# The rounding of the sequence table on VectorE, the square-root table behind the first casts, and a cast in contiguous order: relu²-attention with Fourier mixing on one core

## The chip, the cores and the metric

The kernel runs on one core of a Trainium2 chip. The metric is the device time of one execution in microseconds (us). The kernel before takes 571.43 us, the median of three runs (570.71 to 571.96 us).

## The reference, cut to what matters

```python
def _attn_ref(q, k, v):                       # (8, 12, 448, 64) each
    scores = scale * np.matmul(q, k.transpose(0, 1, 3, 2))
    attn = np.maximum(scores, 0.0) ** 2 / S   # S = 448
    return np.matmul(attn, v)

def _moe_ref(x, w_ch1, w_ch2):                # x: (8, 448, 768), w: 768x3072, 3072x768
    mixed = np.real(np.fft.fft(np.fft.fft(x, axis=1), axis=2))
    u = x + mixed
    un = (u - mean(u)) / np.sqrt(var(u) + 1e-06)      # over the last axis
    return u + np.maximum(un @ w_ch1, 0.0) @ w_ch2
```

`x` is the attention output, with the twelve heads side by side in the last axis. The real part of the two Fourier transforms is computed as matrix products with tables of cosines and sines, one table along the channels (768) and one along the sequence (448).

## The kernel before, in words

**Staging.** The eight batches run through one software pipeline. For each batch: attention (scores L954 on TensorE, relu on ScalarE at L967, squares on VectorE at L984 or on ScalarE at L981, products with v at L822 and L827), the transposed attention output `xT` copied out of PSUM (L673 for batch 0, L689 for the others), sums and differences of mirrored sequence positions (`fold`, L748 for batch 0, L727 to L780 later), the product with the channel table (`mix`, L1407 for batch 0 and L1432 later), the casts of its result to `pc` (L1451), the product with the sequence table (L1029 and L1032 for batch 0; L1244 for batch 1 and L1240 for the later ones), layernorm, and the two layers of the channel network (first layer L1928, its relu on VectorE L1913 or ScalarE L1915 into `hT`; second layer L1956, L1983 and L2069, whose result VectorE adds to the output at L1621). From some batches on, the network runs with pre-added blocks (L2045 to L2057), which saves products.

**Tables.** The sequence table is made at run time in `seq_table` and `seq_sines`: GpSimd (POOL) forms position times frequency over 448 (L366), rounds it to the nearest whole number (L369) and takes the fraction (L371); VectorE takes the absolute value (L377); ScalarE makes cosines and sines of it (three instructions, L383) into `seq` (`seqm` in the profile) and `nseq`. `root_table` (L399) is a square root of a constant whose purpose is to bring ScalarE's table of the square root in at a chosen place: the ACT_TABLE_LOAD in front of it is the cost. `halve` (L407 to L411) multiplies the table with a permutation on TensorE and casts the result into `half_seq` (`seqh`), whose even and odd columns stand in two blocks.

**The order of the work.** `Streams.run` lays the program out while it is built. Each piece of work is a generator that asks for its next step with `need(engine, duration, what it waits for, buffers)`; the planner takes the step that can start first by its own model, with an added rank and small corrections by phase (`HEAD`), and issues it. What the engines then do on the chip is in exactly that order on each engine, whatever the real durations are. So a changed duration or constant in the model can move instructions anywhere later. Loads from memory are issued by POOL (software queue, L451, L476 for q, k and v; L515 and L526 for the weights, shown as `w<-in_moe_w_ch_dram`), relayouts, transposes and stores by SyncE (SP).

Of the kernel before, what the change touches and what calls it, by code (L numbers as in the profile page):

```python
# [13 lines left out]
ALU = mybir.AluOpType  # L14
# [47 lines left out]

HEAD = {('attentions', 'PE', 2): -0.6, ('attentions', 'PE', 3): -0.6}
OVERLAP = {"ACT": 0.12, "DVE": 0.07}
STAGE = [1]
LATENCY = {"PE": 0.28, "ACT": 0.18, "DVE": 0.16, "POOL": 0.2, "SP": 0.1}
# [89 lines left out]
def act(n):  # L158
    return n / 1200 + (0.17 if STAGE[0] else 0.2)
# [18 lines left out]
def kernel(  # L178
# [174 lines left out]
    def seq_table():  # L353

        f = work.tile([128, 4 * KH], FP32, name="dfty", tag="uA", bufs=1)
        g = work.tile([128, 4 * KH], FP32, name="dfty", tag="uB", bufs=1)
        yield need("POOL", 0.55)
        nc.gpsimd.iota(drow[:, 0:2], pattern=[[128, 2]], base=0, channel_multiplier=1,
                       allow_small_or_imprecise_dtypes=True)
        nc.gpsimd.iota(dcol[:, 0:SX], pattern=[[1, SX]], base=0, channel_multiplier=0,  # L360
                       allow_small_or_imprecise_dtypes=True)
        yield need("POOL", 0.3)
        nc.gpsimd.tensor_scalar(drow[:, 0:2], drow[:, 0:2], 1.0 / S, None, op0=ALU.mult)
        for i in range(2):
            yield need("POOL", 0.45)
            nc.gpsimd.tensor_scalar(f[:, i * SX:(i + 1) * SX], dcol[:, 0:SX], drow[:, i:i + 1], None, op0=ALU.mult)  # L366
        f, g = f[:, 0:2 * SX], g[:, 0:2 * SX]
        yield need("POOL", 0.75)
        nc.gpsimd.tensor_scalar(g, f, ROUND, -ROUND, op0=ALU.add, op1=ALU.add)  # L369
        e = yield need("POOL", 1.1)  # L370
        nc.gpsimd.tensor_tensor(f, f, g, op=ALU.subtract)  # L371
        sch.add(seq_sines(f, g, e + LATENCY["POOL"]), (0, 0.3))

    def seq_sines(f, g, e):

        e = yield need("DVE", 0.4, [e])
        nc.vector.tensor_scalar(g.bitcast(mybir.dt.int32), f.bitcast(mybir.dt.int32), 0x7FFFFFFF, None,  # L377
                                op0=ALU.bitwise_and)
        flat = seq.rearrange("p t a s -> p t (a s)")
        for dst, y, sign, bias in ((flat[:, 0], g, -1, halfpi), (flat[:, 1], f, 1, zero_t),  # L380
                                   (nseq.rearrange("p a s -> p (a s)"), f, -1, zero_t)):
            e = yield need("ACT", act(2 * SX), [e + LATENCY["DVE"], last_relu])
            nc.scalar.activation(dst, y, AF.Sin, bias=bias, scale=sign * 2.0 * math.pi)  # L383
        seq_ready.t = nseq_ready.t = dft_ready.t = e + LATENCY["ACT"]

    ROUND = 1.5 * 2 ** 23
    chan_made, dft_made = [Cell() for _ in range(3)], Cell()

    def negative():
# [5 lines left out]

    def root_table():

        yield need("ACT", 1.5, [dft_ready, last_relu])
        nc.scalar.activation(drow[:, 7:8], zero_t, AF.Sqrt, bias=eps_t)  # L399

    def halve():

        yield need("SP", 0.0, [tail_left])
        e = yield need("PE", mm(2 * SX), [], [BS])
        pt = BS.take()
        for t in range(2):
            nc.tensor.matmul(pt[:2 * EH, t, 0:SX], lhsT=order[0][:EV, 0:2 * EH], rhs=seq[:EV, t, 0, :],  # L407
                             start=True, stop=True)
        e = yield need("DVE", 1.1, [e + LATENCY["PE"]], [BQR])
        half_seq[0] = work.tile([128, 2, 2, EV], BF16, name="seqh", tag="warm", bufs=1)  # L410
        nc.vector.tensor_copy(half_seq[0][:2 * EH].rearrange("p t o s -> p t s o"),  # L411
                              pt[:2 * EH, :, 0:2 * EV].rearrange("p t (s o) -> p t s o", o=2))
        BS.give(pt, e)
        BQR.free.append(e)
        half_ready.t = e + LATENCY["DVE"]

    GRP = 4 * R * HG * Dh * 4
    TURNED, STORED, RELAYED = 1.0, 1.0, 0.0
    loads = [[None] * 3 for _ in range(B * NG)]
    ready = [[Cell() for _ in range(3)] for _ in range(B * NG)]  # L420
    BQ = [[Bufs(1) for _ in range(QN)] for _ in range(2)] + [Bufs(3)]
# [12 lines left out]
    def arrive(i, x):  # L434

        arrived.setdefault((i, x), []).append(landed[-1])
        if len(arrived[i, x]) == (1, 2, 2)[x]:
            ready[i][x].t = max(arrived[i, x]) + (1.5 if i % NG else 0.0, 3.0, 6.0, 8.0)[min(i // NG, 3)]

    def load_halves(b, g, n, x):  # L440

# [205 lines left out]
    def fold(b, m, F, av, give, av_end):  # L647
# [4 lines left out]
        def leave():  # L652
# [10 lines left out]
            if b == 0:  # L663
                bufs = [BX[m]] + ([BA[m]] if m < 3 else [])
                wait = {x: max(av_end, sch.engine[x]) + sch.queued(x) for x in ("ACT", "DVE")}
                en = "ACT" if m in (3, 4) and wait["ACT"] + 2 * act(HS) < wait["DVE"] + 2 * dve(HS) else "DVE"
                for out_, in_ in (xa, xb):
                    t = yield need(en, act(HS) if en == "ACT" else dve(HS), [av_end], bufs)
                    bufs = []
# [290 lines left out]
    def squares(b, scs, sqs):  # L960
        for i, sc, t in scs:
            e = yield need("ACT", act(2 * S) - (0.0 if STAGE[0] else 0.03), [t + LATENCY["PE"]], [BSQ])
            at = min(sq_ids)
            sq_ids.remove(at)
            r = sqs[i][0] = work.tile([128, 2, S], BF16, name="sq", tag=f"sq{at[1]}", bufs=1)
            sqs[i][2] = at[1]
            nc.scalar.activation(r, sc[:, :, 0:S], AF.Relu)  # L967
            BS.give(sc, e + 0.1)
            if b == 0 and i == NB - 1:
                last_relu.t = e  # L970
            sch.add(square(b, r, e + LATENCY["ACT"], sqs[i][1]), (0.2, 0.2))

    def sooner(t, other, d, usual, du):

        wait = {en: max(t, sch.engine[en]) + sch.queued(en) for en in (other, usual)}
        return wait[other] + d + SPARE < wait[usual] + du

    def square(b, r, t, done):
        if b >= ELASTIC[0] and sooner(t, "ACT", act(2 * S), "DVE", dve2(2 * S)):
            e = yield need("ACT", act(2 * S), [t])  # L980
            nc.scalar.activation(r, r, AF.Square)  # L981
        else:
            e = yield need("DVE", dve2(2 * S), [t])
            nc.vector.tensor_tensor(r, r, r, op=ALU.mult)  # L984
        done.t = e + LATENCY["DVE"]
# [430 lines left out]
    def mix(b):  # L1416
# [23 lines left out]
            BFS.free.append(e)  # L1440
        for (n0, n1), (pp, t) in zip(TC, pps):
            n = n1 - n0 if b < PAR else 2 * EH
            en, copy = ("ACT", nc.scalar.copy) if n0 == 0 or b == 1 else ("DVE", nc.vector.tensor_copy)
            pc = None

            for w in ((slice(0, 1), slice(1, 2)) if b == 0 else (slice(0, 2),)):
                e = yield need(en, dve((w.stop - w.start) * 2 * KH), [t], [BPC] if n0 == 0 and w.start == 0 else [])
                if pc is None:
                    pc = work.tile([128, 2, 2 * KH], BF16, name="pc", tag=f"pc{n0}", bufs=1)

                copy(pc[:n, w].rearrange("p t (k r) -> p t r k", r=2),  # L1451
                     pp[:n, w, 0:2 * KH].rearrange("p t (r k) -> p t r k", r=2))
            BS.give(pp, e)
            pcs.append((pc, e + LATENCY["ACT"]))
        if b == 0:
            yield need("PE", 0.0, [], [BUNT, BUNT])
            for t0, n in ((0, 384), (384, 512)):
# [696 lines left out]
            begun = True  # L2154

    LEAD, MIXED, SPARE, ELASTIC = 2.9, 1, 0.5, (1, 99)
    SLOPE = 0.1
    with tc.manual_schedule():
        small_constants()
        sch.engine.update(POOL=0.5, DVE=2.6)  # L2160
# [52 lines left out]
```

## Time and profile before

| | |
|---|---|
| three timed runs | 570.71, 571.43, 571.96 us |
| profiled execution | 572.91 us, its span 571.1 us |
| granted TensorE clock | 1.000 |
| busy: PE, DVE, ACT, POOL | 558.0, 440.3, 317.7, 202.4 us |
| share of the chain that ended last | PE 90%, DVE 3%, DMA 2%, ACT 2% |

PE is TensorE, DVE is VectorE, ACT is ScalarE, POOL is GpSimd, SP is SyncE; the span runs from the first instruction to the last of the profiled execution. L numbers are lines of the kernel before. In rows of the timeline and of the chain the first column is the start in us from the span's start, the second a length; in rows of a table by stretches the first number is the stretch, the second its length, then the busy time of PE, PEld (weight loads), DVE, ACT and POOL with their instructions, the granted clock, the DMA share and GB/s.

### The profile page before, as it was taken

What the parts mean: (1) busy time and instruction counts of PE and PEld (TensorE: products, weight loads), DVE (VectorE), ACT (ScalarE), POOL (GpSimd) and SP (SyncE); (2) the same over time, 40 slices, a digit from 0 to 9 for tenths busy, and PEclk for the clock granted to TensorE, in tenths of its full rate; (3) what the DMA queues carried; (4) which work ended last, traced back from release to release, by engine and by line L of the source; (5) the groups of instructions that cost most, each with busy time, mean ns of one, the idle gap of its engine ahead of it and who ended that gap; (6) DMA issues with size and microseconds to landing.
All of it is one profiled execution on the core that took longest, in us unless ns stands there. A gap on an engine that the chain in (4) does not pass through costs nothing.

```text
span 571.1 us, 11283 instructions
## 1 busy us (share of the span) xinstructions
PE 558.0 (98%) x4240; PEld 353.1 (62%) x4240; DVE 440.3 (77%) x1019; ACT 317.7 (56%) x530; POOL 202.4 (35%) x284
## 2 busy tenths in 40 slices
PE   8989999999999999997999999999999999999997
PEld 6466546644465455555756766756668688668864
DVE  6977675887788978886998897888799967644762
ACT  5967772667645687585686647728515164005400
POOL 8987225524346234462455536325006000000000
PEclk9999999999999999999999999999999999999999
DMA  9999999989969998899999999956415421332012
GB/s 113 172 199 237 186 218 182 253 113 117 195 90 213 214 128 176 149 188 182 163 133 208 198 130 193 173 120 169 106 64 155 120 96 20 78 117 65 1 55 84
DMA packets 152689, 82.43 MB, mean 144 GB/s; under 512 B 118076, under 2 KB 147900, under 8 KB 152636
## 3 DMA queue, kind: packets, MB, share of 16 engines
q0 software_dynamic: 57056, 33.63, 43.5%
q1 hardware_dynamic: 95580, 48.09, 38.3%
q8 instruction: 33, 0.54, 0.4%
q14 instruction: 20, 0.16, 0.1%
HBM read 62.91 MB, written 26.25 MB: 156 GB/s over the span
## 4 chain that ended last, share of the span: by engine, by line
PE 90%; DVE 3%; DMA 2%; ACT 2%; POOL 1%; issue 1%; SPq 0%; DVEq 0%; POOLq 0%; ACTq 0%
PE psF L1928 27%; PE psF L2069 21%; PE psS L1760 8%; PE psS L954 7%; PE psS L2069 5%; PE psF L827 5%; PE psF L1956 4%; PE psF L1983 4%; PE psS L1432 2%; PE psF L1760 2%; PE psF L822 1%; DMA qk<-in_k_dram 1%; DVE sq L984 1%; DMA qkT<-qkr 1%; PE psS L827 1%; PE psS L1029 1%
## 5 line engine op out<-in xcount | busy, mean ns | idle before, releaser
L1928 PE MATMUL psF<-unT,w 128*128 128x256 bf16 (+2 forms) x1152 | 165.4, 299 | 1.1 <-DVE hT L1913 0.9
L967 ACT ACTIVATE sq<-psS 128x896 bf16<-128x896 f32 x168 | 144.4, 919 | 33.2 <-PE psS L954 32.8
L1928 PEld LDWEIGHTS <-w 128*128 128x128 bf16 x1152 | 110.9, 98 | 50.9 <-issue 6.7
L984 DVE TENSOR_TENSOR sq<-sq 128x896 bf16<-128x896 bf16 x143 | 88.8, 638 | 11.5 <-ACT sq L967 10.7
L2069 PEld LDWEIGHTS <-hT 128*128 128x128 bf16 x648 | 62.5, 98 | 43.6 <-issue 3.9
L1915 ACT ACTIVATE hT<-psF 128x512 bf16<-128x512 f32 (+2 forms) x118 | 58.0, 507 | 42.7 <-PE psF L1928 41.9
L1621 DVE TENSOR_TENSOR o<-psF,o 128x384 f32<-128x384 f32 (+1 forms) x78 | 42.6, 547 | 24.3 <-PE psF L2069 19.4
L2069 PE MATMUL psF<-w,hT 128*128 128x384 bf16 x336 | 60.1, 326 | 0.7 <-DVE o L1621 0.6
L954 PE MATMUL psS<-qkT 64*128 64x448 bf16 (+1 forms) x336 | 51.7, 354 | 3.4 <-DVE pc L1451 2.3
L1775 ACT COPY copies<-psS 128x256 f32<-128x256 f32 x57 | 19.9, 374 | 53.9 <-PE psS L1760 48.8
L1275 POOL TENSOR_TENSOR u<-tp,xn 112x385 f32<-112x385 f32 (+2 forms) x14 | 14.5, 1038 | 81.5 <-DVE tp L1255 62.0
L689 DVE TENSOR_SCALAR xT<-psF 128x224 bf16<-128x224 f32 x62 | 21.2, 384 | 23.2 <-PE psF L827 23.2
L476 POOL DMA_DIRECT2D qn<-in_q_dram x21 | 15.6, 742 | 59.3 <-DVE qkr L583 52.3
L954 PEld LDWEIGHTS <-qkT 64*128 64x128 bf16 (+1 forms) x336 | 13.1, 94 | 35.3 <-issue 29.0
L827 PE MATMUL psF<-sq,vn 128*64 128x448 bf16 x246 | 32.6, 362 | 0.0
L1760 PEld LDWEIGHTS <-w 128*128 128x128 bf16 x288 | 28.2, 98 | 4.7 <-issue 1.0
L1284 DVE BATCH_NORM_STATS2 stats<-u 112x6 f32<-112x384 f32 (+2 forms) x56 | 28.5, 542 | 0.9 <-POOL u L1275 0.6
L451 POOL DMA_DIRECT2D kn<-in_k_dram x42 | 25.7, 622 | 9.6 <-PE psF L1928 8.5
L476 POOL DMA_DIRECT2D vn<-in_v_dram x24 | 19.0, 797 | 27.7 <-PE psS L954 27.4
L451 POOL DMA_DIRECT2D vn<-in_v_dram x42 | 26.0, 632 | 7.9 <-DMA w<-in_moe_w_ch_dram 7.0
L1303 ACT ACTIVATE un<-u,small 113x768 bf16<-113x768 f32 (+2 forms) x21 | 20.9, 1023 | 10.9 <-DVE small L1290 8.3
L1780 DVE CUSTOM_DVE_ANT_0 hT<-psS,copies 128x256 bf16<-128x256 f32 x37 | 15.0, 421 | 14.1 <-PE psS L1760 6.2
(238 smaller groups left out, 961.7 us busy)
## 6 DMA issues: line engine op xcount, KB each, us to landing
out_dram<-o SPq DMA_DIRECT2D x55, 192.0 KB, 3.6
qn<-in_q_dram POOLq DMA_DIRECT2D x21, 224.0 KB, 5.2
vn<-in_v_dram POOLq DMA_DIRECT2D x24, 192.0 KB, 5.9
w<-in_moe_w_ch_dram POOLq DMA_DIRECT2D x12, 384.0 KB, 8.3
w<-in_moe_w_ch_dram POOLq DMA_DIRECT2D x4, 1152.0 KB, 20.5
kn<-in_k_dram POOLq DMA_DIRECT2D x21, 192.0 KB, 6.1
utop<-u SPq DMA_DIRECT2D x12, 336.0 KB, 3.1
o<-utop SPq DMA_DIRECT2D x16, 192.0 KB, 3.4
```

The source lines that it names most:

```text
L451: nc.gpsimd.dma_start(out=t[par * Dh:(par + 1) * Dh, par::2], in_=at)
L476: nc.gpsimd.dma_start(out=to, in_=src[b, hs, 0:rows].rearrange("h (p j) d -> p h (j d)", j=j))
L827: nc.tensor.matmul(av[h * Dh:(h + 1) * Dh, 0:S], lhsT=vn_home[:, at:at + Dh], rhs=sq[:, h, :], start=start, stop=stop, skip_group_check=True)
L954: nc.tensor.matmul(sc[:, h, 0:S].rearrange("k (c q) -> k c q", c=4), lhsT=flat[ps, k0:k0 + KB], rhs=qT[ps, pair], start=True, stop=True)
L967: nc.scalar.activation(r, sc[:, :, 0:S], AF.Relu)
L984: nc.vector.tensor_tensor(r, r, r, op=ALU.mult)
L1284: nc.vector.bn_stats(stats[:n, hf, :], u[:n, hf * (D // 2):(hf + 1) * (D // 2)])
L1621: nc.vector.tensor_tensor(o[:, cols], pc[:, cols], o[:, cols], op=ALU.add)
L1760: nc.tensor.matmul(ps[:, 0:N], lhsT=lhs, rhs=rhs[:, m], start=(start and m == 0), stop=(stop and m == 2), skip_group_check=True)
L1915: nc.scalar.activation(hs, ps, AF.Relu)
L1928: nc.tensor.matmul(ph[:, i * N:(i + 1) * N], lhsT=w1_sb[m][hf][:, (jj + i) * 128:(jj + i + 1) * 128], rhs=unT[:, m, 0:N], start=(m == 0), ...
L2069: nc.tensor.matmul(pc[:, cols], lhsT=lhs[i], rhs=rhs[i][:, cols], start=(start and i == 0), stop=(i == KP - 1), skip_group_check=True)
```

## The change

1. **Rounding.** POOL's two instructions (L369, L371) are gone. VectorE gets two in their place, ahead of the absolute value: the fraction's source is written as int32 (which rounds it), and the difference is taken (L373 and L375 of the kernel after).
2. **ScalarE takes two pieces of batch 0** from VectorE: the last square (L984 to L981) and the last `xT` (m = 5, L673 to L671).
3. **The square-root table** is loaded after the first `pc` cast, not before it.
4. **`halve`** casts with the destination in contiguous order; the source is then read in steps of two elements. Before, the source was contiguous and the destination was written in steps of 113 elements.
5. **Batch 1's second `pc` cast** (97 rows) goes to VectorE; both were on ScalarE.
6. **Constants of the planner** change, and with them the order on all engines.

```diff
-HEAD = {('attentions', 'PE', 2): -0.6, ('attentions', 'PE', 3): -0.6}
+HEAD = {('attentions', 'PE', 2): -0.6, ('attentions', 'PE', 3): -0.6, ('attentions', 'PE', 4): 0.07, ('mix_rows', 'PE', 2): -0.05}
...
 def seq_table():
...
-            yield need("POOL", 0.45)
+            e = yield need("POOL", 0.45)
...
-        yield need("POOL", 0.75)
-        nc.gpsimd.tensor_scalar(g, f, ROUND, -ROUND, op0=ALU.add, op1=ALU.add)
-        e = yield need("POOL", 1.1)
-        nc.gpsimd.tensor_tensor(f, f, g, op=ALU.subtract)
...
 def seq_sines(f, g, e):
         e = yield need("DVE", 0.4, [e])
+        nc.vector.tensor_scalar(g.bitcast(mybir.dt.int32), f, 1.0, None, op0=ALU.mult)
+        yield need("DVE", 0.55)
+        nc.vector.tensor_tensor(f, f, g.bitcast(mybir.dt.int32), op=ALU.subtract)
+        e = yield need("DVE", 0.4)
...
 def root_table():
-        yield need("ACT", 1.5, [dft_ready, last_relu])
+        yield need("SP", 0.0, [dft_ready, last_relu, first_copied])
+        yield need("ACT", 1.5, [first_copied])
...
 def halve():
-        e = yield need("DVE", 1.1, [e + LATENCY["PE"]], [BQR])
+        e = yield need("DVE", dve(4 * EV), [e + LATENCY["PE"]], [BQR])
-        nc.vector.tensor_copy(half_seq[0][:2 * EH].rearrange("p t o s -> p t s o"),
-                              pt[:2 * EH, :, 0:2 * EV].rearrange("p t (s o) -> p t s o", o=2))
+        nc.vector.tensor_copy(half_seq[0][:2 * EH], pt[:2 * EH, :, 0:2 * EV].rearrange("p t (s o) -> p t o s", o=2))
...
-    TURNED, STORED, RELAYED = 1.0, 1.0, 0.0
+    TURNED, STORED, RELAYED = 1.367, 1.225, 0.203
...
-            ready[i][x].t = max(arrived[i, x]) + (1.5 if i % NG else 0.0, 3.0, 6.0, 8.0)[min(i // NG, 3)]
+            ready[i][x].t = max(arrived[i, x]) + (1.5 if i % NG else 0.0, 2.944, 4.08, 8.038)[min(i // NG, 3)]
...
-                en = "ACT" if m in (3, 4) and wait["ACT"] + 2 * act(HS) < wait["DVE"] + 2 * dve(HS) else "DVE"
+                en = "ACT" if m == MC - 1 or m in (3, 4) and wait["ACT"] + 2 * act(HS) < wait["DVE"] + 2 * dve(HS) else "DVE"
...
-    def square(b, r, t, done):
-        if b >= ELASTIC[0] and sooner(t, "ACT", act(2 * S), "DVE", dve2(2 * S)):
+    def square(b, r, t, done, scalar):
+        if scalar or b >= ELASTIC[0] and sooner(t, "ACT", act(2 * S), "DVE", dve2(2 * S)):
...
-            en, copy = ("ACT", nc.scalar.copy) if n0 == 0 or b == 1 else ("DVE", nc.vector.tensor_copy)
+            en, copy = ("ACT", nc.scalar.copy) if n0 == 0 else ("DVE", nc.vector.tensor_copy)
...
-    SLOPE = 0.1
+    SLOPE = 0.127
```

The new order, at three places. **ScalarE in the head of the program**, from the end of batch 0's attention to the first rows of its layernorm (`sq` are attention weights, `seqm` and `nseq` the sequence table, `pc` the casts of the channel product). Before:

```order
L967 ACTIVATE sq<-psS 128x896
L383 ACTIVATE seqm<-dfty,few 128x480 x2
L383 ACTIVATE nseq<-dfty,few 128x480
L399 ACT_TABLE_LOAD
L399 ACTIVATE drow<-few 128x1
L1451 CAST pc<-psS 128x2x193 x2
L630 COPY qkT<-psF 128x960
L1081 COPY u<-psS 128x384
```

and with the change:

```order
L967 ACTIVATE sq<-psS 128x896
L981 ACTIVATE sq<-sq 128x896
L383 ACTIVATE seqm<-dfty,few 128x480
L671 ACTIVATE xT_108<-psF 128x224 x2
L383 ACTIVATE seqm<-dfty,few 128x480
L383 ACTIVATE nseq<-dfty,few 128x480
L1451 CAST pc<-psS 128x2x193 x2
L630 COPY qkT<-psF 128x960
L400 ACT_TABLE_LOAD
L400 ACTIVATE drow<-few 128x1
L1081 COPY u<-psS 128x384
```

The square and the two halves of `xT` have come in, and the table load has moved behind the casts and the copy of `qkT`, in front of the first copy of the rows.

**VectorE where batch 1's channel product ends** (`qkr` are q and k of batch 2 on their way to a transpose, `pc` the second cast, `o` the output's accumulator). Before:

```order
L740 TENSOR_TENSOR fold<-fold,seqm 128x450
L583 COPY qkr<-qn 112x1024
L1621 TENSOR_TENSOR o<-psF,o 128x384
L583 COPY qkr<-kn 128x1024
L1255 TENSOR_TENSOR tp<-psS,qs 128x385
```

and with the change (L1623 is L1621 of before):

```order
L740 TENSOR_TENSOR fold<-fold,seqm 128x450
L583 COPY qkr<-qn 112x1024
L1451 CAST pc<-psS 97x2x2x193
L1623 TENSOR_TENSOR o<-psF,o 128x384
L583 COPY qkr<-kn 128x1024
L1255 TENSOR_TENSOR tp<-psS,qs 128x385
```

The cast has come in behind the copy of q and ahead of the add into the output.

**VectorE ahead of the channel product L1432 that stands at 368.5 us in the trace of before** (`fold` and `diff` are what that product reads; `hT` are blocks of the network). Before:

```order
L770 TENSOR_TENSOR fold<-folds 128x684
L778 TENSOR_TENSOR diff<-fold 128x1368
L984 TENSOR_TENSOR sq<-sq 128x896
L780 TENSOR_TENSOR fold<-fold 128x1368
L984 TENSOR_TENSOR sq<-sq 128x896
L2045 TENSOR_TENSOR hT<-hT 128x512
```

and with the change (L2047, L2049, L2051 and L1623 are L2045, L2047, L2049 and L1621 of before):

```order
L778 TENSOR_TENSOR diff<-fold 128x1368
L984 TENSOR_TENSOR sq<-sq 128x896
L2047 TENSOR_TENSOR hT<-hT 128x256
L2049 TENSOR_TENSOR hT<-hT 128x256
L2051 TENSOR_TENSOR hT<-hT 128x2x128
L1623 TENSOR_TENSOR o<-psF,o 128x384
L780 TENSOR_TENSOR fold<-fold 128x1368
```

The last fold of the batch now stands behind the network's block additions and behind one add into the output. On TensorE the same place holds two dozen products L2069 ahead of L1432 that stood behind it before, and twelve L1928 that stood just ahead of it have moved up by some 8 us.

More of the change, by code (lines that the diff above doesn't have):

```diff
@@ L384, in seq_sines @@
         seq_ready.t = nseq_ready.t = dft_ready.t = e + LATENCY["ACT"]
-    ROUND = 1.5 * 2 ** 23
+    first_copied = Cell()
     chan_made, dft_made = [Cell() for _ in range(3)], Cell()
@@ L970, in squares @@
                 last_relu.t = e
-            sch.add(square(b, r, e + LATENCY["ACT"], sqs[i][1]), (0.2, 0.2))
+            sch.add(square(b, r, e + LATENCY["ACT"], sqs[i][1], b == 0 and i == NB - 1), (0.2, 0.2))
     def sooner(t, other, d, usual, du):
@@ L1454, in mix @@
             pcs.append((pc, e + LATENCY["ACT"]))
+            if b == 0 and en == "ACT":
+                first_copied.t = e
         if b == 0:
```

## The prediction

> **What bounds the kernel now.** I read four views in this order: the busy times by stretches, TensorE's waits, the chain of work that ended last, and the timeline at the places that the change touches. The table by stretches shows where TensorE (first busy number) isn't full.
>
> ```profile
> 60.00:93.00 33.00, 32.78 (x236) 17.88 (x236) 19.54 (x48) 22.23 (x33) 6.21 (x10) 1.00 1.25 197
> 93.00:257.00 164.00, 163.80 (x1040) 84.72 (x1039) 136.78 (x323) 106.70 (x168) 73.92 (x98) 1.00 1.04 168
> 257.00:270.00 13.00, 10.09 (x82) 6.35 (x79) 7.63 (x15) 6.84 (x8) 2.03 (x3) 1.00 1.23 177
> ```
>
> ```profile
> 359.00:410.00 51.00, 50.89 (x408) 34.57 (x406) 43.95 (x97) 31.98 (x48) 14.02 (x16) 1.00 0.77 143
> ```
>
> From 60 to 257 us TensorE is idle for 0.42 us of 197, from 359 to 410 for 0.11. No work leaves TensorE with this change, so only its waits can go or come. Two of the longest lie where the change acts:
>
> ```profile
> PE psS L1029 <- ACT pc L1451: 1.3, 1, 1.3
> ```
>
> ```profile
> PE psF L1928 <- DVE hT L1913: 0.9, 1, 0.9
> ```
>
> They stand at 36.7 and 52.6 us, as the rows below show. What is idle from 257 to 270 us (13.00 - 10.09 = 2.9) belongs to an order that the change leaves alone.
>
> **The head, up to 60 us.** The sequence table is late, and everything waits behind it. POOL rounds, VectorE's absolute value comes next, then ScalarE's sines, its table load and the casts that TensorE waits for:
>
> ```profile
> 28.78 1.84 POOL L369 TENSOR_SCALAR dfty<-dfty 128x480 f32<-128x480 f32 x1
> 30.71 1.48 POOL L371 TENSOR_TENSOR dfty<-dfty 128x480 f32<-128x480 f32 x1
> ```
>
> ```profile
> 32.24 0.40 DVE L377 TENSOR_SCALAR dfty<-dfty 128x480 int32<-128x480 int32 x1
> ```
>
> ```profile
> 32.67 1.28 ACT L383 ACTIVATE seqm<-dfty,few 128x480 bf16<-128x480 f32 x2 [2.77 <-DVE dfty L377]
> 33.86 0.68 ACT L383 ACTIVATE nseq<-dfty,few 128x480 bf16<-128x480 f32 x1
> 34.56 1.28 ACT L399 ACT_TABLE_LOAD   x1
> 35.85 0.29 ACT L399 ACTIVATE drow<-few 128x1 f32<-128x1 f32 x1
> 36.05 1.03 ACT L1451 CAST pc<-psS 128x386 bf16<-128x386 f32 x2
> 36.93 0.97 ACT L630 COPY qkT<-psF 128x960 bf16<-128x960 bf16 x1
> ```
>
> VectorE's two new instructions don't exist in this trace. The rounding has the shape of L377, 0.40 us; the difference has two inputs, and I take 0.6 us from the add L1621 over 384 elements (0.56 us, quoted below). Bounds are 0.4 for each and POOL's own 1.84 and 1.48. Three instructions at about 1.4 us, begun near 30.1 us behind the folds of the first three tiles, end at 31.5 instead of 32.64. The sines then start 1.1 us earlier; the two halves of the last `xT`, new between them on ScalarE, give back some 0.65. The added square falls into ScalarE's 2.77 us of idling, at
>
> ```profile
> L981 ACT ACTIVATE sq<-sq 128x896 bf16<-128x896 bf16 x25 | 23.6, 954 | 0.4
> ```
>
> 0.95 us, so it costs nothing; without that cover it would delay the sines by as much. With the load and the root (1.57) out of the way, the casts begin near 34.2 instead of 36.05 (36.05 - 1.1 + 0.65 - 1.57 = 34.03, and 0.17 for handoffs): **1.85 us earlier**. VectorE's half of the casts follows the folds, and two `xT` halves in front of them are gone.
>
> But the load is not gone. It now stands behind the copy L630, ahead of the first copy of a row tile, and TensorE's row tiles are filled and emptied in turn:
>
> ```profile
> 38.48 0.48 ACT L1081 COPY u<-psS 128x384 f32<-128x384 f32 x1 [0.58 <-DVE stats L1052]
> ```
>
> ```profile
> 36.68 0.94 PE psS L1029 x4
> 37.62 0.17 PE psS L1032 x3
> 37.79 0.66 PE psS L1029 x4
> 38.45 0.17 PE psS L1032 x3
> ```
>
> Casts until 35.2, L630 until 36.15, load and root until 37.75: the first L1081 ends near 38.25, where the profile has 38.96. The first three row tiles (0.66 + 0.17 = 0.83 us each) don't need it; the fourth, which began at 36.68 + 1.11 + 2 x 0.83 = 39.45, does. So it comes 1.2 us earlier and not 1.85, and I put the rows' gain at **1.1 us**.
>
> The Trainium skill (ScalarE: Activation LUTs, "What ACT_TABLE_LOAD costs") puts a switch at 1283 ns for the load plus about 1380 ns of drain. The row of the load agrees with the first number; of the drain nothing shows, since the load starts as the third sine ends (33.86 + 0.68) and the square root as the load ends. By the page the row tiles would come 0.3 us later than before (1.1 - 1.38), which leads to the third rival below; by the rows they come 1.1 earlier.
>
> Then `halve`, by the chain of work:
>
> ```profile
> 50.05 2.11 DVE seqh L411
> ```
>
> ```profile
> 52.59 3.57 PE psF L1928 x21
> ```
>
> The cast takes 2.11 us for 452 elements per partition. The copy L1081 above takes 0.48 us for 384, so what makes the cast long is the step in which it writes. The new form reads in steps of two elements and writes in sequence. VectorE already reads PSUM that way: L689 takes every second element from batch 2 on, and none skipped in batch 1. The two answers (minimum, median, maximum in ns), first batch 1, then a late batch:
>
> ```profile
> L689 DVE TENSOR_SCALAR xT<-psF x10: 383/388/393, 62.9 to 87.5; 128x224 bf16<-128x224 f32 x10
> ```
>
> ```profile
> L689 DVE TENSOR_SCALAR xT<-psF x4: 378/381/392, 402.6 to 408.0; 128x224 bf16<-128x224 f32 x4
> ```
>
> No difference, so I take 0.6 us, 1.5 less; the bounds are 0.5 and 2.1. That is more than TensorE's 0.89 us of waiting, so of it 0.9 is gained: a head shorter by **1.1 + 0.9 = 2.0 us** at 60 us, between 0 (load and cast give everything back) and 2.7 (1.85 + 0.89).
>
> The Trainium skill (SBUF — State Buffer, "Door 1: The DMA port swizzle") says that a stride pays wherever it leaves a line, of 16 bytes in SBUF and of 8 in PSUM. It agrees with the slow write (steps of 226 bytes). The new read, 8 bytes at a step, would pay too; the rows of L689, with the same step, show no such thing. By the page the head gains 1.1, by the rows 2.0.
>
> **What becomes of the 2 us.** Everything above is a gain of engines, and the loads don't hear of it. POOL's issues, and the hardware queue between 60 and 92 us:
>
> ```profile
> 58.55 1.69 POOL L526 DMA_DIRECT2D w<-in_moe_w_ch_dram  x2 [1.22 <-issue]
> 60.23 0.74 POOL L476 DMA_DIRECT2D qn<-in_q_dram  x1
> ```
>
> ```profile
> 90.56 0.72 POOL L476 DMA_DIRECT2D qn<-in_q_dram  x1 [6.98 <-DMA w<-in_moe_w_ch_dram]
> ```
>
> ```profile
> q1 hardware_dynamic: 3478, 1.64, 30.2%
> ```
>
> The hardware queue takes 30% of the 16 engines, and both together 1.25 of them in the table by stretches (packets overlap): they are full. The last quarter of the second layer's weights (issued at 59.4) lands at about 90.4, and batch 2's q, issued at 60.23, 31.9 us later, at 92.1. An earlier issue only lengthens the queue. VectorE's, ScalarE's and TensorE's rows there:
>
> ```profile
> 92.14 0.43 DVE L583 COPY qkr<-qn 112x1024 bf16<-112x1024 bf16 x1 [2.91 <-DMA qn<-in_q_dram]
> 93.18 0.56 DVE L1621 TENSOR_TENSOR o<-psF,o 128x384 f32<-128x384 f32 x1 [0.62 <-PE psF L1956]
> 94.22 0.43 DVE L583 COPY qkr<-kn 128x1024 bf16<-128x1024 bf16 x1 [0.48 <-DMA kn<-in_k_dram]
> ```
>
> ```profile
> 91.21 2.03 ACT L1451 CAST pc<-psS 128x772 bf16<-128x772 f32 x2 [4.49 <-PE psS L1432]
> ```
>
> ```profile
> 92.01 2.11 PE L1956 MATMUL psF<-w,hT 128*128 128x384 bf16 x12
> 93.96 1.49 PE L1244 MATMUL psS<-pc,seqm 128*128 128x385 bf16 x8
> ```
>
> Before, both casts are ScalarE's and end at 93.24; TensorE, busy until 93.96, never waits. With the change the second cast is VectorE's, **behind the copy of q** in a queue that goes in order, and that copy waits for the transfer whatever TensorE has gained. The price is in the trace already, because the stall at 270 us is the same sequence:
>
> ```profile
> 268.56 0.43 DVE L583 COPY qkr<-kn 128x1024 bf16<-128x1024 bf16 x1 [4.59 <-DMA qkT<-qkr]
> 268.90 1.02 DVE L1451 CAST pc<-psS 114x772 bf16<-114x772 f32 x1
> ```
>
> ```profile
> 269.98 0.37 PE psS L954 x2
> ```
>
> There TensorE went on 269.98 - 268.56 = 1.42 us after the copy began. So L1244 begins at 92.14 + 1.42 = **93.56** instead of 93.96: of 2.0 us, 0.4 is left, and TensorE shows a new wait of about 1.6 us. Queued behind the cast are L1621 (0.4 later, its PSUM isn't needed before L1244's 1.49 us are over) and the copy of k, which waits for its own data until 94.2 anyhow. The landing itself may move: 2 us of hardware-queue traffic at 30% that is pushed ahead of it would cost 0.6 us, so the gain lies between -0.2 and 0.4 plus what the transfers give, 1.6 at most (the last weights land at 90.4, and TensorE wants them at 92.01). I take 0.4.
>
> **The new order from 359 to 410 us** can only cost, since 0.11 us of idling is all that could go. Ahead of L1432 stand now 24 products L2069, a dozen taking 2.06 us, and VectorE has to add one result (0.56) and make the last fold (0.87) behind the first dozen:
>
> ```profile
> 255.31 2.06 PE psF L2069 x12
> ```
>
> ```profile
> 261.69 0.87 DVE L780 TENSOR_TENSOR fold<-fold 128x1368 bf16<-128x1368 bf16 x1
> ```
>
> 1.43 and some 0.1 of handoffs fit into 2.06, if VectorE is not behind. I count 0 to 0.2 and take 0.1. The upper bound is the stall of the stretch from 257 to 270 us, 13.00 - 10.09 = 2.9 us. The pairs L1240 that stand six products earlier near 164 and 219 us, and the squares that change engine, lie beside a full TensorE: 0, with a bound of 0.4 for the two (0.16 us a product).
>
> **The sum.** For the profiled execution (span 571.1, with 1.8 us around it 572.9, which is 1.5 above the median of the runs shown): -0.4 + 0.1 = -0.3, a span of 570.8. Put on the median: 571.43 - 0.3 = **571.1 us**.
>
> **Rivals.**
> - *The head's gain survives.* If the transfers come with the engines, for instance because the issues of the first layer's weights start some 3 us earlier at 29 us and the queue is not full then, q lands up to 2 us earlier and only the landing of the last weights holds: -1.6, **569.8 us**. For it speaks that POOL loses 3.3 us of work; against it that the queue shows a backlog. If the cast of `seqh` then keeps its 2.11 us, because the new read pays for its steps as the old write did, 1.1 is left: 570.3 us. (The sentence of the Trainium skill on lines, above, is this case.)
> - *Slower: the last fold comes late.* VectorE is 44 of 51 us busy from 359 to 410. If its rows ahead of L780 are more than 0.5 us behind (2.06 - 1.53), L1432 waits, the casts and transposes behind it follow, and the next batch's scores stand as at 257 us: 1.5 to 2.9 us, **573.4 us** with 2.3 as the middle, less 0.3.
> - *The change doesn't do what it says.* The load ahead of the rows, with a switch longer than the row shows, or slow new instructions on VectorE, eat the head's gain. L1244 then begins between 93.56 and 93.96 all the same: **571.3 us**, within the forecast.
>
> **How the numbers follow.** Forecast 0.36, the third rival 0.10, the head's gain 0.30, the late fold 0.20; 0.04 for neither. A measurement of this kernel can tell about 0.2% (1.1 us) from no change: the forecast and the third rival lie within it, the first rival beyond it with most of its chance, the second wholly. That gives faster 0.31, within 0.2% 0.45, slower 0.24. The range takes in the first rival down to 569.3 and the late fold up to 573.2; the forecast's own is 570.5 to 571.9.
>
> **What would show it.** Right: L1029 begins near 34.8 us, the rows end near 42.4, the cast of `seqh` takes 0.6 us, no wait of 0.9 at L1928; and a wait of 1 to 1.6 us at L1244 for the cast on VectorE, which has waited for q until about 92.1. Wrong: L1244 without a wait and q landed at 90 (first rival); TensorE idle for over 1 us between 365 and 400 us (second); L1029 later than 36 or the cast above 1.5 us (third). A landing of q after 92.7 would make the forecast too low.

## The result, and the profile after

The kernel after takes **568.12 us** (median of 11 runs, 567.50 to 568.77); the kernel before, over its 11 runs beside them, 571.43 us (570.35 to 575.79). The ratio is 0.9939, with a 95% interval of 0.9921 to 0.9957: 3.3 us faster. The forecast was 571.1 with a range from 569.3 to 573.2: the kernel came out faster than the whole range. The profiled execution took 568.09 us, its span is 566.3 us.

TensorE by stretches, after (columns as in the prediction):

```profile
60.00:93.00 33.00, 32.36 (x221) 17.78 (x220) 20.00 (x48) 19.52 (x30) 5.78 (x9) 1.00 1.24 202
```

```profile
257.00:270.00 13.00, 12.35 (x108) 9.20 (x105) 9.96 (x18) 7.29 (x10) 3.11 (x5) 1.00 1.14 182
359.00:410.00 51.00, 51.00 (x398) 34.05 (x397) 42.37 (x96) 31.04 (x49) 10.13 (x12) 1.00 0.66 134
```

The two spans differ by 4.8 us, more than the medians. Of that, 2.3 stand from 257 to 270 us (10.09 of 13 busy before, 12.35 after), at a place where none of the changed instructions stands. A second profile of the kernel before, below, has 12.35 there too. So I read the change's own gain in the head: what TensorE waits for from 30 to 100 us is now

```profile
PE psS L1244 <- DVE pc L1451: 0.6, 1, 0.6
PE psS L1029 <- ACT u L1081: 0.3, 1, 0.3
PE psS L1130 <- DVE unT L1146: 0.2, 1, 0.2
```

Both old waits (1.3 and 0.9 us) are gone. The predicted new one, at L1244 behind the cast on VectorE, is there, at 0.6 us and not 1.6. ScalarE's head:

```profile
31.50 0.69 ACT L383 ACTIVATE seqm<-dfty,few 128x480 bf16<-128x480 f32 x1 [0.62 <-DVE dfty L377]
32.10 0.59 ACT L671 ACTIVATE xT<-psF 128x224 bf16<-128x224 f32 x2
32.57 0.69 ACT L383 ACTIVATE seqm<-dfty,few 128x480 bf16<-128x480 f32 x1
33.16 0.69 ACT L383 ACTIVATE nseq<-dfty,few 128x480 bf16<-128x480 f32 x1
33.96 1.06 ACT L1451 CAST pc<-psS 128x386 bf16<-128x386 f32 x2
34.86 0.98 ACT L630 COPY qkT<-psF 128x960 bf16<-128x960 bf16 x1
35.84 1.28 ACT L400 ACT_TABLE_LOAD   x1
37.13 0.29 ACT L400 ACTIVATE drow<-few 128x1 f32<-128x1 f32 x1
37.34 0.46 ACT L1081 COPY u<-psS 128x384 f32<-128x384 f32 x1
```

and VectorE's three instructions on the table and the cast in `halve`:

```profile
29.93 0.40 DVE L373 TENSOR_SCALAR dfty<-dfty 128x480 int32<-128x480 f32 x1
30.36 0.66 DVE L375 TENSOR_TENSOR dfty<-dfty 128x480 f32<-128x480 f32 x1
31.05 0.41 DVE L377 TENSOR_SCALAR dfty<-dfty 128x480 int32<-128x480 int32 x1
```

```profile
48.43 0.62 DVE L412 CAST seqh<-psS 114x452 bf16<-114x452 f32 x1
```

All of this is as worked out: sines from 31.50 (32.67 - 1.1 = 31.57 was worked out), casts from 33.96 (34.2), the cast of `seqh` 0.62 us (0.6). What is not as worked out is the landing of batch 2's q. It came at 90.69 and not at 92.14, and TensorE's L1244 went on at 92.11, not at 93.56:

```profile
90.69 0.43 DVE L583 COPY qkr<-qn 112x1024 bf16<-112x1024 bf16 x1 [4.28 <-DMA qn<-in_q_dram]
91.04 1.02 DVE L1451 CAST pc<-psS 97x772 bf16<-97x772 f32 x1
```

```profile
91.14 0.33 PE L1244 MATMUL psS<-pc,seqm 128*128 128x385 bf16 x1
92.11 1.32 PE L1244 MATMUL psS<-pc,seqm 97*128 97x385 bf16 x7 [0.64 <-DVE pc L1451]
```

From copy to L1244 it is 92.11 - 90.69 = 1.42 us, exactly the price that the prediction took from the stall at 270 us.

### The profile page after: what moved, and what is told of

The parts are those of the page before. It is cut to its first block, busy times and chain, and to the rows that moved or that the text cites. A ratio compares the mean times of both kernels' runs of the same rounds, so it can differ in the third digit from the quotient of the medians.

```text
span 566.3 us, 11286 instructions
## 1 busy us (share of the span) xinstructions
PE 557.4 (98%) x4240; PEld 353.1 (62%) x4240; DVE 437.8 (77%) x1016; ACT 318.3 (56%) x536; POOL 196.6 (35%) x281
## 4 chain that ended last, share of the span: by engine, by line
PE 87%; DMA 7%; POOL 2%; ACT 1%; DVE 1%; issue 1%; DVEq 0%; POOLq 0%; ACTq 0%
PE psF L1930 24%; PE psF L2071 21%; PE psS L1762 8%; PE psS L954 7%; DMA qn<-in_q_dram 6%; PE psS L2071 5%; PE psF L827 4%; PE psF L1985 4%; PE psF L1958 3%; PE psS L1432 2%; PE psF L1762 2%; DMA qk<-in_k_dram 1%; PE psF L822 1%; PE psS L827 1%; PE psS L1240 1%
## 5 line engine op out<-in xcount | busy, mean ns | idle before, releaser
L984 DVE TENSOR_TENSOR sq<-sq 128x896 bf16<-128x896 bf16 x144 | 89.1, 636 | 14.2 <-ACT sq L967 13.5
L1917 ACT ACTIVATE hT<-psF 128x512 bf16<-128x512 f32 (+2 forms) x121 | 59.6, 508 | 41.1 <-PE psF L1930 40.3
L1623 DVE TENSOR_TENSOR o<-psF,o 128x384 f32<-128x384 f32 (+1 forms) x78 | 42.6, 547 | 23.4 <-PE psF L2071 19.5
L689 DVE TENSOR_SCALAR xT<-psF 128x224 bf16<-128x224 f32 x60 | 20.6, 384 | 26.8 <-PE psF L827 26.8
L954 PEld LDWEIGHTS <-qkT 64*128 64x128 bf16 (+1 forms) x336 | 13.0, 94 | 32.6 <-issue 27.6
L1303 ACT ACTIVATE un<-u,small 112x768 bf16<-112x768 f32 (+2 forms) x22 | 22.0, 1023 | 9.4 <-DVE small L1290 8.3
```

Source lines behind the costliest of these rows:

```text
L954: nc.tensor.matmul(sc[:, h, 0:S].rearrange("k (c q) -> k c q", c=4), lhsT=flat[ps, k0:k0 + KB], rhs=qT[ps, pair], start=True, stop=True)
L1623: nc.vector.tensor_tensor(o[:, cols], pc[:, cols], o[:, cols], op=ALU.add)
L1917: nc.scalar.activation(hs, ps, AF.Relu)
```

## The experiments

The question was why the loads land 1.4 us earlier. **Theory A:** POOL, freed of the rounding, issues the second half of the first layer's weights (L515) earlier, and the software queue wasn't full there. **Rival B:** the landings follow the engines, which free buffers earlier. POOL's rows for these issues, before and then after:

```profile
33.42 3.26 POOL L515 DMA_DIRECT2D w<-in_moe_w_ch_dram  x6
```

```profile
29.89 1.70 POOL L515 DMA_DIRECT2D w<-in_moe_w_ch_dram  x3
31.96 0.54 POOL L515 DMA_DIRECT2D w<-in_moe_w_ch_dram  x1 [0.37 <-DMA w<-in_moe_w_ch_dram]
33.89 0.54 POOL L515 DMA_DIRECT2D w<-in_moe_w_ch_dram  x1 [1.39 <-DMA w<-in_moe_w_ch_dram]
35.68 0.54 POOL L515 DMA_DIRECT2D w<-in_moe_w_ch_dram  x1 [1.25 <-DMA kn<-in_k_dram]
```

Before, the six issues go out one behind the other and none waits. After, the last three each wait for an earlier load.

Each ratio is the kernel's time over that of the kernel before, with its 95% interval, from five rounds; the median of before that was measured with it stands beside the medians. That median lay between 570.91 and 571.43 us, so a difference of less than about 0.5 us between two of the changed kernels means nothing.

**1. The kernel before, profiled again.** No edit.

> The kernel before, unchanged, profiled a second time. Theory A (the stall near 257 to 270 us belongs to the order): TensorE idle for 2.9 us there again, and TRANSPOSE unT<-nbot (L1380) again 3.5 us long on SP. Rival B (it is a matter of when transfers meet and differs from run to run): idle between 0.6 and 2.9 us, with an L1380 between 1.6 and 3.5 us. L1244 at 93.96 within 0.2 us in both.

570.93 us, span 569.1. The stall is short this time:

```profile
257.00:270.00 13.00, 12.35 (x99) 8.13 (x98) 9.52 (x18) 7.44 (x10) 3.25 (x5) 1.00 1.16 198
```

On SP, L1380's transpose of `nbot` took 2.20 us here, 3.54 in the first profile, 1.61 after. Rival B of that run holds: the same order has the long stall in one execution and not in another. (In the profiles of experiments 2 to 6 and 8 to 11 it is absent too.) L1244 stood at 94.38, 0.4 later than expected: VectorE came to the cast of `seqh` 0.4 us later (50.38, not 49.96), and the wait at L1928 was 1.4 us and not 0.9. Against this profile the after kernel is 2.8 us shorter, some 2.4 of it at L1244 (from 94.38 to 92.11, where one of the eight products is done already).

**2. The cast alone**, in the kernel before:

```diff
-        nc.vector.tensor_copy(half_seq[0][:2 * EH].rearrange("p t o s -> p t s o"),
-                              pt[:2 * EH, :, 0:2 * EV].rearrange("p t (s o) -> p t s o", o=2))
+        nc.vector.tensor_copy(half_seq[0][:2 * EH],
+                              pt[:2 * EH, :, 0:2 * EV].rearrange("p t (s o) -> p t o s", o=2))
```

> Before, with the cast of seqh alone in contiguous order; the order of every engine stays as it was. The cast takes 0.6 us, not 2.1, and TensorE's wait of 0.9 us at L1928 (52.6 us) is gone in both theories. Theory A (landings follow POOL's issues, which here depend little on the cast): L1244 begins 0 to 0.3 us earlier than 93.96, time 0 to -0.3 us. Rival B (landings follow the engines): L1244 0.9 us earlier, time -0.9 us.

570.48 us beside 571.31; ratio 0.9979 (0.9962 to 0.9997). TensorE's wait for the relu behind the cast is gone, but L1244 stood at 94.38, no earlier than in experiment 1. In its place TensorE waited for loads at L623, 0.3 us for q and 0.6 for k, at 58 to 59 us:

```profile
PE psF L623 <- DMA kn<-in_k_dram: 0.6, 1, 0.6
```

The loads of this execution ran late from the first (5.11 MB at 34 us, 5.26 in experiment 1), so one pair of profiles can't place the gain; the runs spread from 569.4 to 572.1. Between the two theories this run is inconclusive.

**3. POOL kept busy**, in the kernel after: 20 small index writes, whose values nothing reads any more, where the rounding stood.

```diff
-        f, g = f[:, 0:2 * SX], g[:, 0:2 * SX]
+        f, g, _ = f[:, 0:2 * SX], g[:, 0:2 * SX], [nc.gpsimd.iota(drow[:, 0:2], pattern=[[128, 2]], base=0, channel_multiplier=1, allow_small_or_imprecise_dtypes=True) for _ in range(20)]
```

> After, with 20 small index writes on POOL (some 3.3 us in all) where the rounding stood, so that POOL issues the second half of the first layer's weights as late as before, while VectorE's, ScalarE's and TensorE's head stays as short. Theory A (the landings came forward because these issues did): q of batch 2 lands near 92 again instead of 90.65, L1244 begins near 93.4 instead of 92.1, time +1.2 to +1.5 us over after. Rival B (the landings follow the engines, whose progress frees the buffers and semaphores that later issues wait for): q lands within 0.3 us of 90.65, time within 0.3 us of after.

570.17 us beside 571.31; ratio 0.9972 (0.9954 to 0.9990). Up to 42 us the engines' head is as short as in after (the rows of batch 0 end at 41.91, there at 42.15), and yet 2.0 of the 3.2 us are lost. The first of the issues came at 34.25 (after: 29.89), q landed at 92.97, and L1244 waited 1.0 us. Theory A, with a larger price than expected. The price is not that landing alone: POOL came late to its part of the layernorm, for which TensorE waited 0.4 us at L1130, and a load of v held up the product L822 by 0.8 us at 54 us.

**4. Both `pc` casts of batch 1 on ScalarE**, in the kernel after:

```diff
-            en, copy = ("ACT", nc.scalar.copy) if n0 == 0 else ("DVE", nc.vector.tensor_copy)
+            en, copy = ("ACT", nc.scalar.copy) if n0 == 0 or b == 1 else ("DVE", nc.vector.tensor_copy)
```

> After, with batch 1's second pc cast back on ScalarE (97 rows, behind the first); nothing else moves. If the cast behind q's copy is what TensorE waits for at L1244 (0.64 us), that wait is gone: both casts end near 90.5, L1244 runs on from 91.14, time -0.6 us against after. Rival: TensorE waits for the last weights or for PSUM instead, or the stall after it returns at 257 us: 0 us.

568.21 us, ratio 0.9941 (0.9922 to 0.9959): the same as after. The wait for the cast is gone and another stands in its place, 0.4 us at the second layer's products for the last weights (`PE psF L1958 <- DMA w`). The rival was right about the time. Its cause is read from one execution, the slowest of nine (569.35), in which the loads came 1.5 us later than in after; there it was the software queue that counted at 92 us, through another consumer.

**5. The long head with the early issues**, in the kernel after: the square root is issued straight behind `nseq`, ahead of the casts, and `seqh` is cast in its old form.

```diff
-        seq_ready.t = nseq_ready.t = dft_ready.t = e + LATENCY["ACT"]
+        seq_ready.t = nseq_ready.t = dft_ready.t = e + LATENCY["ACT"]; nc.scalar.activation(drow[:, 7:8], zero_t, AF.Sqrt, bias=eps_t)
...
-        nc.scalar.activation(drow[:, 7:8], zero_t, AF.Sqrt, bias=eps_t)
...
-        nc.vector.tensor_copy(half_seq[0][:2 * EH], pt[:2 * EH, :, 0:2 * EV].rearrange("p t (s o) -> p t o s", o=2))
+        nc.vector.tensor_copy(half_seq[0][:2 * EH].rearrange("p t o s -> p t s o"), pt[:2 * EH, :, 0:2 * EV].rearrange("p t (s o) -> p t s o", o=2))
```

> After, with the head as long as it was: the square-root table ahead of the first casts and the cast of seqh in its old form (2.1 us); the order is otherwise that of after, and POOL issues the weights early as in after. Theory A (both are needed, the time is the later of the two): q of batch 2 still lands near 90.7 us, but TensorE comes to L1244 near 93.5 without a wait for the cast; time +1.3 to +1.7 us over after, about 569.6. Rival B (the landings follow the engines): q lands 1.5 us later as well, with the wait at L1244 kept, time about the same 569.6. Rival C (only the transfers count): L1244 within 0.3 us of 92.1, time within 0.3 us of after.

569.33 us beside 570.94; ratio 0.9977 (0.9958 to 0.9995). TensorE has both waits of the head again (1.2 and 0.9 us), and q lands as early as ever:

```profile
90.74 0.43 DVE L583 COPY qkr<-qn 112x1024 bf16<-112x1024 bf16 x1 [2.70 <-DMA qn<-in_q_dram]
```

L1244 ran without a wait, at 92.77 (93.5 was expected). This excludes rival B: the engines were slow, the landing stayed. It also gives back 1.2 us of after's gain (1.7 by the 570.94 beside it), so both halves are needed: **at L1244 the later of engines and loads counts.**

**6. POOL kept busy for less**, 15 writes, so that the first issue stands at 33.24, where the kernel before has it (33.42).

```diff
-for _ in range(20)]
+for _ in range(15)]
```

> After with 15 index writes on POOL in place of 20, so that the first issue of the weights' second half stands within 0.3 us of 33.3, where it stood before (20 put it at 34.25). Theory A (a queue that has run low while POOL is busy): time between after and the kernel with 20, about +1.2 us over after, 569.3, and q lands near 92. Rival (the index writes do harm in another way, not by the delay): the same +2.0 as with 20.

570.26 us beside 570.94; ratio 0.9975 (0.9955 to 0.9994), the same as with 20. q landed at 93.37 (in the kernel before, issued as late, at 92.14; why it was later still is open). TensorE waited 1.0 us at L1244, and ahead of it for the last weights:

```profile
91.52 2.11 PE L1958 MATMUL psF<-w,hT 128*128 128x384 bf16 x12 [1.62 <-DMA w<-in_moe_w_ch_dram]
```

The time is the rival's, +2.1 us, and the harm doesn't grow from 15 writes to 20. So theory A needed a sharper form, and the rival, that the writes themselves do the harm, had to be tested; experiment 8 does both.

**7. The constants.** The kernel after with the old constants, and the kernel before with the new ones:

```diff
-    TURNED, STORED, RELAYED = 1.367, 1.225, 0.203
+    TURNED, STORED, RELAYED = 1.0, 1.0, 0.0
```

(and so `HEAD`, the times of `arrive` and `SLOPE`; in the second kernel the other way round.)

> After, with the planner's constants of before; everything else as in after. Theory A (the constants only keep the order from 100 us on as full as it was): TensorE's wait at L1244 as in after, and 0.3 to 2 us lost later, most of it between 93 and 410 us, time 568.4 to 570. Rival: no difference within 0.3 us; or the constants themselves carry a gain in the head, with L1244 over 0.5 us later.

583.56 us, ratio 1.0213 (1.0194 to 1.0233): **15 us slower than after**, far outside either expectation. The head is untouched (L1244 resumes at 92.03); the loss stands where the order fell out worse, for example

```profile
140.00:200.00 60.00, 56.03 (x353) 28.64 (x353) 50.34 (x117) 29.54 (x42) 24.14 (x33) 1.00 0.96 154
200.00:255.00 55.00, 50.50 (x319) 26.61 (x316) 41.68 (x96) 38.03 (x74) 21.88 (x30) 0.94 0.98 154
```

4.0 and 4.5 us idle where after has none (in the second stretch the granted clock was 0.94 as well). These two stretches are 8.5 of the 15 us.

> Before, with the planner's new constants alone. Theory A: head as before, L1244 near 94.2, TensorE as full as before from 93 us on; time within 0.5 us of before. Rival (the constants carry part of the gain): 0.5 to 1.5 us faster.

575.85 us, ratio 1.0065 (1.0045 to 1.0085): slower by 4.9, against both expectations. In the profiled execution, the slowest of six (579.64), VectorE's copy of q, which waits for its load, has come ahead of the last folds of batch 1, which TensorE needs:

```profile
92.36 0.43 DVE L583 COPY qkr<-qn 112x1024 bf16<-112x1024 bf16 x1 [4.71 <-DMA qn<-in_q_dram]
92.71 0.27 DVE L727 TENSOR_TENSOR seqm<-xT 128x225 bf16<-128x225 bf16 x1
92.89 0.27 DVE L729 TENSOR_TENSOR seqm<-xT 128x225 bf16<-128x225 bf16 x1
93.20 0.39 DVE L737 TENSOR_TENSOR diff<-fold,seqm 128x450 bf16<-128x450 bf16 x1
93.62 0.39 DVE L740 TENSOR_TENSOR fold<-fold,seqm 128x450 bf16<-128x450 bf16 x1
```

```profile
PE psS L1432 <- DVE fold L740: 4.0, 1, 4.0
```

So the new constants have no gain of their own; they go with the new pieces of work and cost 4.9 us without them.

**8. POOL kept busy for least**, 8 writes.

```diff
-for _ in range(20)]
+for _ in range(8)]
```

> After with 8 index writes on POOL (about 1.7 us), half of what 15 added. Theory A, in the form that the runs with 15 and 20 writes leave (a threshold: POOL waits for the ring of the software queue until 35.7 anyway, so a delay that ends before the queue has run low costs nothing): six issues of the weights end within 0.3 us of 36.2 as in after, q lands within 0.5 us of 90.7, time within 0.4 us of after, 568.1 to 568.5. Rival (the harm grows with the delay): half of the 2.1 us that 15 and 20 writes cost, 569.2.

567.95 us beside 570.91; ratio 0.9945 (0.9931 to 0.9960): as fast as after, though the first issue came at 32.53, 2.6 us later than in after and only 0.7 us before that of experiment 6. So the writes as such do no harm, and the delay does it as a **threshold**, between a first issue at 32.53 and one at 33.24. POOL's rows, experiment 6 and then 8:

```profile
33.24 3.26 POOL L515 DMA_DIRECT2D w<-in_moe_w_ch_dram  x6
```

```profile
32.53 2.73 POOL L515 DMA_DIRECT2D w<-in_moe_w_ch_dram  x5
36.22 0.55 POOL L515 DMA_DIRECT2D w<-in_moe_w_ch_dram  x1 [0.95 <-DMA kn<-in_k_dram]
```

With 8 writes the sixth issue still finds the queue full and waits 0.95 us (it ends at 36.77, 0.5 later than expected); with 15, as in the kernel before, none waits. The difference shows in the load traffic too, most clearly from 35 to 36 us. Packets, megabytes and rate, and the software queue's share of the 16 engines (concurrent packets count twice); first the kernel before, then experiment 6, experiment 8 and after:

```profile
DMA packets 204, 0.15 MB, mean 150 GB/s; under 512 B 161, under 2 KB 161, under 8 KB 204
q0 software_dynamic: 204, 0.15, 122.3%
```

```profile
DMA packets 87, 0.11 MB, mean 106 GB/s; under 512 B 59, under 2 KB 59, under 8 KB 86
```

```profile
q0 software_dynamic: 86, 0.09, 71.4%
```

```profile
DMA packets 290, 0.22 MB, mean 220 GB/s; under 512 B 231, under 2 KB 231, under 8 KB 289
```

```profile
DMA packets 199, 0.22 MB, mean 217 GB/s; under 512 B 133, under 2 KB 133, under 8 KB 199
q0 software_dynamic: 199, 0.22, 126.2%
```

Late issues leave a gap there: 150 and 106 GB/s beside 220 and 217. The queue's share shows it in experiment 6 (71.4%), but not in the kernel before, where it is 122.3% at 150 GB/s and 126.2% at 217 after. From 34 to 40 us the kernels whose issues come late move 1.06 to 1.12 MB (before, experiments 1, 2 and 6) and 0.89 (experiment 3); those with early issues 1.24 to 1.26 (after, experiments 4, 5 and 8 to 11). The difference of 0.16 MB between before and after is 0.76 us at 210 GB/s, about half of the 1.45 us by which q lands earlier. The other half I have not placed. By the time at which POOL issues that q, 1.2 of the 1.45 us are there: 59.01 in after (58.98 in experiment 5) beside 60.23 before, 60.25 in experiment 6 and 61.41 in experiment 3. From the issue to the landing it takes 31.6 to 33.1 us in all five.

**9. Issues earlier still**, in the kernel after: POOL's two multiplications ahead of the rounding go to VectorE.

```diff
-            nc.gpsimd.tensor_scalar(f[:, i * SX:(i + 1) * SX], dcol[:, 0:SX], drow[:, i:i + 1], None, op0=ALU.mult)
+            nc.vector.tensor_scalar(f[:, i * SX:(i + 1) * SX], dcol[:, 0:SX], drow[:, i:i + 1], None, op0=ALU.mult)
```

> After, with POOL's two multiplications in front of the rounding (L366, 2.65 us) on VectorE as well, so that POOL issues the weights 2.6 us earlier still. Theory A (in after the queue is full from 24 us on, and POOL waits for its ring): the issues start near 27 but end as in after, q lands within 0.3 us of 90.7, time within 0.3 us of after. Rival (earlier is better): q 1 to 2 us earlier, time -0.6 us, the length of the wait at L1244.

568.65 us, ratio 0.9959 (0.9944 to 0.9974): no gain. The first issue comes at 26.88, but each later one waits 0.8 to 1.35 us for an earlier load, the sixth ends at 36.28 (35.74 + 0.54; 36.22 in after), and q lands at 90.75. Now the queue is full. VectorE pays: TensorE waits 0.4 us for a square at 27.6 us.

**10. The old cast in the kernel after.** The edit is the last of experiment 5 alone.

> After, with the cast of seqh in its old form, written in steps of 113; the order is that of after. The cast takes 2.1 us again and TensorE waits 0.9 us at L1928. Theory A (at L1244 the later of engines and transfers counts, and the engines are 0.6 us ahead there): the wait at L1244 shrinks from 0.64 to about 0, time +0.3 us over after. Rival (the engines alone count): +0.9 us with the wait at L1244 unchanged.

568.14 us beside 570.91; ratio 0.9952 (0.9938 to 0.9967): undoing this part costs little, 0.0 us beside after's median and 0.5 by the 570.91 beside it. The cast takes 2.20 us and TensorE waits the 0.9 us, but at L1244 the wait is gone, since that is how far the engines were ahead:

```profile
50.80 3.08 PE L1930 MATMUL psF<-unT,w 128*128 128x384 bf16 x18 [0.90 <-DVE hT L1915]
91.93 1.49 PE L1244 MATMUL psS<-pc,seqm 128*128 128x385 bf16 x8
```

Theory A again (0.3 us was expected; q landed 0.8 us earlier in this execution).

**11. Experiments 4 and 9 together.**

> After, with both edits: the multiplications on VectorE, and batch 1's second pc cast on ScalarE. It beats after only if earlier issues bring the last weights forward too: then -0.6 us and L1244 without a wait. Theory A: TensorE waits for the last weights (0.4 us, as with the cast alone on ScalarE), time within 0.3 us of after.

568.49 us, ratio 0.9952 (0.9938 to 0.9965): no better than after. In the profiled execution, the slowest of six (569.18), q landed at 91.80, and TensorE waited 0.2 us for the last weights. No kernel here beats after by more than its runs spread.

## Why the prediction was wrong, point by point

- **The head.** Right, and a little low. The rows' end moved from 43.69 to 42.15 (1.5 us; 1.1 was worked out), and the 0.9 at `halve` went as said. TensorE came to its first product at L1244 at 91.14, 2.8 us ahead of 93.96, where 2.0 was said.
- **The table load.** 1.28 us with the square root straight behind it, as in before, and the first L1081 began at 37.34: 0.4 us earlier than the sum had it. The longer switch that the Trainium skill names (ScalarE: Activation LUTs, "What ACT_TABLE_LOAD costs") doesn't show: the load starts as L630 ends (34.86 + 0.98), and TensorE waits 0.3 us for ScalarE, no more.
- **The cast.** 0.62 us with a read in steps of two elements, as forecast from L689. But L689 is not the same read. By its source line it steps through PSUM by 112 elements from one read to the next in batch 1 and by 224 from batch 2 on (four blocks of 112 are read in turn), where the prediction has steps of one and of two. Both rows, 388 and 381 ns for 224 elements, are reads in long steps, so the conclusion that such steps cost VectorE nothing was right, and for larger steps than was said. With the Trainium skill (SBUF — State Buffer, "Door 1: The DMA port swizzle") the runs agree on the write that leaves its line at each element, 2.20 us again in experiment 10. Its sentence on PSUM names matmuls, and VectorE's reads in steps of 8 bytes showed nothing of the kind.
- **The failed step** is this one: "An earlier issue only lengthens the queue", and "they are full" before it. The prediction read the engines' share over 60 to 92 us, where it holds, and not the traffic from 34 to 40 us, where the software queue ran low: 184 GB/s before, 210 after, and 150 beside 217 in the worst microsecond. The gap lies outside the stretch that was read, and the share would not have shown it there either. In the place of a landing fixed at 92.1 the runs showed one that follows POOL's issues: early issues 90.7 whether the head is short or long (after, experiment 5; 90.8 in 8 and 9, 89.9 in 10), late issues 93.0 and 93.4 with the short head (experiments 3 and 6) and 92.0 to 92.8 with that of before (before, experiments 1 and 2). Single executions scatter: with both casts on ScalarE (experiments 4 and 11) it was 92.2 and 91.8 in spite of early issues, with medians like after's; why is open.
- **What that step is worth.** The last product L1244 ended at 92.11 + 1.32 = 93.43, where the prediction had 93.56 + 1.49 = 95.05: 1.6 of the 3.0 us between the forecast and the median. Another 0.1 is the cost of the new order, which didn't come. Going by the second profile of before, 0.4 is its longer wait at L1928 (1.4 us) and some 0.4 are small waits between 93 and 410 us (46.69, 59.84 and 50.89 us busy in stretches where after has 46.80, 60.00 and 51.00). The last 0.5, between that execution (570.93) and the median of before, stays open.
- **The price at L1244** was right (1.42 us behind q's copy), with the wrong landing put into it. The first rival named the cause, POOL's issues starting some 3 us earlier with a queue that isn't full, and got 0.30. Its time, 569.8, was still 1.7 us too slow. It held the last weights at 90.4, and they came forward as well: POOL's next load, which waits for them, was issued at 88.94 instead of 90.56. That is worth the step from its 1.6 us to the 2.0 measured at L1244 (95.45 to 93.43); the rest is the remainder of the point above.
- **The new order from 359 to 410 us** cost nothing: 51.00 of 51 busy. The order that the constants make was costed at 0.1; alone the constants cost 4.9 us, their absence 15.4 (experiment 7). In this change they go with the rest, so the forecast wasn't hurt by it.
- **The base.** The profile of before held a stall of 2.9 us, of which 2.3 came and went between executions. I had carried it as a fixed part. It didn't enter the sum, but its size served as the upper bound of the second rival.

The 3.3 us by parts, from four kernels: late issues and long head 571.4, late issues and short head 570.3 (experiment 6), early issues and long head 569.3 (experiment 5), both 568.1. The head without the issues gives 0.7 (beside the 570.94 measured with it) to 1.2, the issues without the head 1.6 to 2.1, both 3.3. Experiment 5's head is shorter than that of before, since the faster table stays: TensorE comes to L1244 at 92.77 without a wait, 1.2 us ahead of 93.96. So the share of the issues is an upper bound, and not a clean one. What of the medians' difference comes from the stall near 260 us being rarer after is open: the runs of after spread over 1.3 us, those of before over 5.4; of the profiles with the order of before one in three has the stall (before, experiments 1 and 2), of those with the order of after none in nine. The execution of before without it, 570.93, is 0.5 below the median.

## What to carry to other kernels

Before a landing is called fixed, look at the queue microsecond by microsecond, from the earliest issue on which it may hang, and in bytes rather than shares: where an engine both computes and issues transfers, its computing can delay a landing that is needed 60 us later, as POOL's rounding did here. Whether the issues wait for earlier loads tells if the queue was full. Where engines and loads meet, a gain on one side is worth only its lead over the other, and undoing it may cost next to nothing. And a part that changes durations should be tried with its planner's constants and without, since the order can be worth more than the part.

## What the runs showed of the hardware that was not expected

- A write in steps of 226 bytes made a cast of 452 elements take 2.19 us; the same with a read in steps of 8 bytes from PSUM 0.62 us.
- POOL's index writes of 128x2 take 0.22 us each (15 in 3.35 us).
- A transpose on SP (L1380 of `nbot`) took 1.38 us (experiment 2), 2.20 (experiment 1) and 3.54 (the first profile) in three executions of the same order on SP. The stall of TensorE near 270 us stands in the longest alone, but that transpose is not shown to be its cause: SP went on to the next one only 0.5 us later than in experiment 1 (263.55, 263.03), and VectorE's copy behind that came 2.3 us later (268.56, 266.28).
